# Batch 0's squares first, four norm products, q scales through DRAM, and another order of loads, in a channel-attention and MLP kernel

## The chip, the cores and the metric

The kernel runs on one core of one Trainium2 chip. The metric is the device time of one execution in microseconds (us), as the median of several runs. Differences of about 0.2% (4.3 us) are what a measurement of this kernel can tell from no change.

## The reference

Four batches of `q`, `k`, `v` with 6080 rows and 256 channels go through channel attention, and its result through a two-layer MLP of width 2048 with an activation that is a clipped square:

```python
qn = q / (norm(q, axis=1) + 1e-6);  kn = k / (norm(k, axis=1) + 1e-6)   # (B, N, C)
s = kn.transpose(0, 2, 1) @ qn / tau                                    # (B, C, C)
a = softmax(s, axis=-1)
x = (v @ a).reshape(B * N, C)
h = x @ w_in
g = where(h >= 1, h, where(h <= -1, 0, (h + 1)**2 / 4))
out = g @ w_out
```

All is float32. The norms run over the 6080 rows, so a batch's softmax needs its whole Gram matrix `k^T q` and the sums of the squares of all its `k` and `q`.

## The kernel before

`v @ a @ w_in` is computed as `v @ (a @ w_in)`, so per batch the kernel makes a matrix W for each of 8 parts of the hidden width (`make_W`, `make_W2`), and then runs 48 blocks (6 pairs of row tiles times 8 parts). A block (`h_ops`, `o_ops`) multiplies W by pieces V of `v` with a seven-product scheme for 2x2 blocks, applies the activation on ScalarE and VectorE, and multiplies by `w_out`. Every product of two float32 numbers is made of three fp32r matmuls of a high and a low half (`mm3`, line 452). There are 192 blocks in all.

An `Order` object collects all operations with an engine, an estimated duration and a due time, and then writes out the order of the instructions by a list schedule: at each step the engine that can start first takes, among the operations that are ready by then, the one with the lowest due time. Due times at or below -1000 (`URGENT`) may also hold their engine up to 0.6 us. After that each engine runs its instructions in the order written, and so does SP's queue of DMAs, which issues every load and store. An instruction whose input is late holds up all behind it on its engine.

The start of the program is a stage of its own. Batch 0's Gram matrix is made from 13 chunks of `kq` (lines 807 to 834) with plain fp32 matmuls (line 818): a chunk has 4 row groups (the first and the last one 2), a row group 2 matmuls of 128x256, and each such matmul stands as two rows in the trace. Four buffers of 1 MB hold chunks, and each becomes free when TensorE and ScalarE have read it. ScalarE squares each chunk in pieces of 1024 columns (lines 826 and 832) and VectorE adds the pieces up in `mh_mem` (line 833, 23 additions). `norm_sums` (line 839) then sums over the partitions with 8 matmuls against one column of ones. `softmax` (line 499) follows: a copy, a power on GpSimd, three small VectorE steps, then the scales of `q` as a row on all partitions (lines 524 to 535: multiply the identity by the scales, multiply by a matrix of ones on TensorE, copy back), the scaled matrix, its maximum, the exponential, four transposes, and the halves of `eT`. `make_W` and the first block come next. The softmax of the other three batches runs inside the blocks of the batch before them, 7 blocks from its end.

Beside that chain the start has work with no link to it: 7 chunks of batch 1's Gram matrix, line 818 too, which TensorE takes as filler (`FILL`, `FSTEP` are its due times), and `convert` (lines 394 to 422), which turns 8 blocks of `w_in` and 8 of `w_out` into halves. One conversion is 3 instructions on ScalarE and 6 on VectorE, and needs one of five `raw` buffers until it has read the block. The list `STARTUP` gives for each block, and for the first V, a due time and the chunk after whose load its own load may be issued. In every batch V needs two `raw` buffers.

Of the kernel before, what the change touches and what calls it, by code (L numbers as in the profile page):

```python
# [8 lines left out]
F32 = mybir.dt.float32  # L9
# [3 lines left out]
AF = mybir.ActivationFunctionType  # L13
ALU = mybir.AluOpType
AX = mybir.AxisListType
P = 128
# [33 lines left out]
URGENT = -1000.0  # L50
# [8 lines left out]
class Order:  # L59
# [28 lines left out]
    def op(self, eng, dur, fn, r=(), w=(), due=0.0, gates=(), size=0, other=None, psum=False, plain=False):  # L88

        o = Op()  # L90
        o.eng, o.dur, o.fn, o.due, o.gates, o.size = eng, dur, fn, due, [g for g in gates if g], size
        o.psum, o.plain = psum, plain
        o.alts = {eng: (dur, fn)}
        if other:
            o.alts[other[0]] = other[1:]
        o.start = o.end = None
        deps = []
        for b in r:
            if b.writer is not None:
                deps.append(b.writer)  # L100
        for b in w:
            deps += b.readers
            if b.writer is not None:
                deps.append(b.writer)
        for b in r:
            b.readers.append(o)
        for b in w:
            b.readers, b.writer = [], o
        o.bufs = list({id(b): b for b in (*r, *w)}.values())
        o.bufs += list({id(b.pool.all): b.pool.all for b in o.bufs if b.pool and b.pool.all}.values())  # L110
        for b in o.bufs:
            b.users.append(o)
            b.left += 1
        o.deps = list({id(d): d for d in deps if d is not o}.values())
        o.next, o.n = [], len(self.ops)
        self.ops.append(o)
        return o
# [114 lines left out]
def act_us(n):  # L232
    return 0.095 + 0.00083 * n


def dve_us(n):
    return 0.067 + 0.00104 * n
# [6 lines left out]
def pool_us(n):  # L244
# [10 lines left out]

EARLY = 7
STARTUP = (
    ('v', 0, -478.3, 15),
    ('out', 5, -462.9, 17),
    ('out', 0, -306.5, 11),  # L260
    ('in', 2, -105.4, 16),
    ('in', 0, -82.1, 7),
    ('in', 1, -62.6, 6),
    ('out', 1, -4.4, 16),
    ('out', 6, 123.4, 7),
    ('out', 2, 163.6, 13),
    ('out', 7, 334.1, 17),
    ('out', 3, 371.7, 3),
    ('out', 4, 467.6, 12),
)  # L270
V_SPREAD = 2.5
WARM = 8
STORE = 15
IN3 = False
WIN_DUE = 41.7
W_DUE = -16.6
FILL = 16.7
FSTEP = -0.13
FIRST = 10
V1 = -7.1  # L280
V1S = 23.8
TAU = 0

# [1 line left out]
def channel_attention_moe(ctx: ExitStack, tc: tile.TileContext, kq, kqT, vT, tau, w_in, w_out, outT):  # L287
# [12 lines left out]
    nc = tc.nc  # L300
    B, N, _, C = kq.shape
# [77 lines left out]
    pools["h22"].held = [acc_all]  # L379
    pools["win2"].held = [win_all]  # L380
    win_dram = [dram.tile([P, 2 * WIN], U32, name=f"win_d{i}") for i in range(FP // 2)]
    w_dram = [[dram.tile([P, WSZ], U32, name=f"w_d{b}_{i}") for i in range(FP)] for b in range(B)]

    ctx.enter_context(tc.manual_schedule())

    def buf(pool):
        return Buf(pools[pool])

    def load(b, src, dst, due, size, gates=(), r=()):
        return op("SP", 0.45, lambda: nc.sync.dma_start(out=dst(), in_=src()), r=r, w=[b], due=due, gates=gates,  # L390
                  size=size)
# [96 lines left out]
    def square_piece(b, s, ct, k, due, gates):  # L488
# [7 lines left out]
                                                               accum_out=st.ssq.ap[:, j:j + 1]),  # L496
           w=[rb, st.ssq], due=due)

    def softmax(b, due):

        st = sts[b]
# [15 lines left out]
        op("DVE", 0.1, lambda: V.tensor_scalar(out=nrm()[:, :CT], in0=nrm()[:, :CT], scalar1=tau_sb[:, 1:2], scalar2=None,  # L517
                                              op0=ALU.mult), r=[tau_buf], w=[c], due=due)
        op("DVE", 0.1, lambda: V.reciprocal(rn(), nrm()), w=[c], due=due)
        d, q, s = (buf("y") for _ in range(3))  # L520
        dd = lambda: d.ap[:, :CT * P].rearrange("p (i c) -> p i c", i=CT)
        ss = lambda: s.ap.rearrange("p (i c) -> p i c", i=CT)
        for ct in range(CT):
            op("DVE", 0.25, lambda ct=ct: V.tensor_scalar(out=dd()[:, ct, :], in0=ident,
                                                         scalar1=rn()[:, CT + ct:CT + ct + 1], scalar2=None,
                                                         op0=ALU.mult), r=[c], w=[d], due=due)
        z = buf("Z")

        def scales():
            od.uneven(3)  # L530
            for ct in range(CT):
                nc.tensor.matmul(z.ap[:, ct * P:(ct + 1) * P], lhsT=ones, rhs=dd()[:, ct, :], start=True, stop=True)  # L532

        op("PE", 0.7, scales, r=[d], w=[z], due=due + 3)
        op("DVE", 0.42, lambda: V.tensor_copy(q.ap[:, :C], z.ap[:, :C]), r=[z], w=[q], due=due + 3)
        gm = (lambda: st.g.ap) if b else (lambda: st.g.ap.rearrange("p (i c) -> p i c", i=CT))
        for it in range(CT):
            op("DVE", 0.42, lambda it=it: V.scalar_tensor_tensor(
# [268 lines left out]
    def big_chunk(i, b, r0, p, T):  # L807
        rb, g = Buf(kq_early), (st.g, g1)[b]
        due = at(0.87 * (r0 // P) + 4) if b == 0 else FILL + FSTEP * (i - n0)
        kq_ops.append(load(rb, lambda: kq[b, r0:r0 + p * T].rearrange("(p t) s c -> p (t s c)", t=T),  # L810
                           lambda: rb.ap[:p, :T * 512], due - 25 if b == 0 else at(56), p * T * 2048,
                           [kq_ops[n0 - 1]] if b else ()))
        last = i == (n0 if b == 0 else len(big)) - 1
        for t in range(T):
            def mm(t=t):
                for it in range(CT):
                    k0 = t * 512 + it * P
                    nc.tensor.matmul(g.ap[:, it * C:(it + 1) * C], lhsT=rb.ap[:p, k0:k0 + P],
                                     rhs=rb.ap[:p, t * 512 + C:t * 512 + 2 * C], start=(r0 == 0 and t == 0 and it == 0),
                                     stop=(last and t == T - 1 and it == CT - 1), skip_group_check=True)  # L820

            op("PE", CT * 0.433, mm, r=[rb], w=[g], due=due, plain=True)
        if b:
            return
        if i == 0:
            op("ACT", act_us(1024), lambda: nc.scalar.activation(acc.ap, rb.ap[:, :1024], AF.Square), r=[rb], w=[acc],
               due=due)
            return
        for t in range(0, T, 2):
            src = lambda t=t: rb.ap[:p, t * 512:t * 512 + 1024]  # L830
            sq = Buf(sq_early)
            op("ACT", act_us(1024), lambda sq=sq, src=src: nc.scalar.activation(sq.ap[:p], src(), AF.Square), r=[rb], w=[sq], due=due)  # L832
            op("DVE", dve_us(1024), lambda sq=sq: nc.vector.tensor_tensor(  # L833
                out=acc.ap[:p], in0=acc.ap[:p], in1=sq.ap[:p], op=ALU.add), r=[sq], w=[acc], due=due)

    def norm_sums():
        for j in range(2 * CT):
            for h in range(2):
                nc.tensor.matmul(st.pt.ap[:, j:j + 1], lhsT=acc.ap[:, h * 512 + j * P:h * 512 + (j + 1) * P],
                                 rhs=ones[:, 0:1], start=(h == 0), stop=(h == 1))  # L840

    def mark_b():

# [10 lines left out]
       w=[tau_ps], due=at(TAU), plain=True)  # L854
    op("DVE", 0.1, lambda: nc.vector.tensor_copy(tau_sb[:, 1:2], tau_ps.ap[:, 0:1]), r=[tau_ps], w=[tau_buf], due=at(TAU))
    st.pt = buf("Z")
    op("PE", 1.84, norm_sums, r=[acc], w=[st.pt], due=URGENT - 20, plain=True)
    softmax(0, URGENT - 20)
    sts[1].g = buf("gacc")
    op("DVE", dve_us(512), lambda: nc.vector.tensor_copy(sts[1].g.ap.rearrange("p i c -> p (i c)"), g1.ap), r=[g1],  # L860
# [73 lines left out]
```

## Time and profile before

| | |
|---|---|
| median of 3 runs | 2154.58 us (2154.46 to 2154.76) |
| profiled execution, its own time | 2155.51 us |
| span in the profile, first to last instruction | 2153.7 us |
| TensorE busy | 2148.7 us of the span |
| VectorE busy | 1785.9 us |
| ScalarE busy | 1634.4 us |
| GpSimd busy | 5.1 us |
| mean granted TensorE clock | 0.999 |

A row of the timeline gives the start, the time covered, the engine, line, operation, the tiles written and read, and how many instructions are merged in it. Matmuls are pipelined, so a single one shows a duration longer than the time after which the next may start: a run of rows covers (number - 1) x pace + the duration of the last. What TensorE loses is therefore read from the starts of runs and not from its busy time. In the lists of engines PE is TensorE's matmuls, DVE VectorE, ACT ScalarE, POOL GpSimd, and SPq the DMA queue of SP.

### The profile page before, as it was taken

The page shows a single profiled execution, that of the slowest core. Times are in us where ns is not written, and L with a number is a line of the kernel's source. Part 1 is how long each engine was busy: PE and PEld are TensorE (multiplying, and loading weights), DVE is VectorE, ACT ScalarE, POOL GpSimd, SP SyncE. Part 2 cuts the span into 40 slices and gives each one's busy share as a digit, 9 for nine tenths or more (in the row PEclk, how much of TensorE's full clock was granted, in tenths as well). Part 3 has the DMA queues.
Part 4 walks back from the last instruction along what each step waited for, and adds up shares of the span by engine and source line. Part 5 has one row for each costly group of instructions (what it writes and reads, how often), then busy time and mean ns, then how long its engine had stood idle before and what let it go on. Part 6 is the DMA issues. An engine that isn't in the chain of part 4 may idle for free.

```text
span 2153.7 us, 27733 instructions
## 1 busy us (share of the span) xinstructions
PE 2148.7 (100%) x9949; PEld 1811.1 (84%) x9949; DVE 1785.9 (83%) x3125; ACT 1634.4 (76%) x2926; POOL 5.1 (0%) x12
## 2 busy tenths in 40 slices
PE   9999999999999999999999999999999999999999
PEld 8888888888888888888888888888888888888887
DVE  8897877888888888888888888888888878878776
ACT  7798877776788777777778877777767777766766
POOL 0000000000000000000000000000000000000000
PEclk9999999999999999999999999999999999999999
DMA  9755445454255444444425445454443432332331
GB/s 381 275 189 188 150 157 173 142 174 148 84 210 190 164 166 152 177 161 161 146 102 211 163 159 183 152 194 152 153 144 118 151 125 91 126 125 100 125 118 37
DMA packets 81467, 340.09 MB, mean 158 GB/s; under 512 B 8370, under 2 KB 16690, under 8 KB 77490
## 3 DMA queue, kind: packets, MB, share of 16 engines
q1 hardware_dynamic: 81330, 338.33, 44.3%
q8 instruction: 78, 1.28, 0.2%
q14 instruction: 59, 0.48, 0.1%
HBM read 279.84 MB, written 58.46 MB: 157 GB/s over the span
## 4 chain that ended last, share of the span: by engine, by line
PE 96%; DVE 2%; DMA 2%; ACT 1%; issue 0%; SPq 0%; DVEq 0%; ACTq 0%
PE bank L452 96%; DMA raw<-w_in 1%; DVE mh_mem L833 1%; DMA raw<-w_out 0%; DMA kq<-kq 0%; ACT u L405 0%; DVE u L415 0%; ACT u L408 0%; DVE sf_mem L575 0%; DVE u L710 0%; ACT sf_mem L832 0%; DVE w_mem L581 0%; DVE u L419 0%; DVE u L406 0%; PE bank L532 0%
## 5 line engine op out<-in xcount | busy, mean ns | idle before, releaser
L452 PE MATMUL bank<-x,wout 128*128 128x512 f32 (+1 forms) x3951 | 1012.9, 387 | 0.2 <-DVE x L714 0.2
L452 PEld LDWEIGHTS bank<-x,wout 128*128 128x128 f32 x3951 | 738.2, 188 | 143.6 <-DVE x L714 0.6
L452 PE MATMUL bank<-v,w_mem 128*128 128x512 f32 (+1 forms) x3264 | 846.5, 387 | 0.0
L452 PEld LDWEIGHTS bank<-v,w_mem 128*128 128x128 f32 x3264 | 611.8, 188 | 120.9 <-DVE u L710 0.5
L710 DVE SCALAR_TENSOR_TENSOR u<-bank,u 128x512 f32<-128x512 f32 (+1 forms) x576 | 391.8, 681 | 236.1 <-ACT u L708 235.3
L706 ACT ACTIVATE u<-bank 128x512 f32<-128x512 f32 (+1 forms) x576 | 342.9, 595 | 226.2 <-PE bank L452 214.3
L708 ACT ACTIVATE u<-u 128x512 f32<-128x512 f32 (+1 forms) x768 | 459.7, 624 | 9.4
L714 DVE TENSOR_TENSOR x<-u,x 128x512 fp32r<-128x512 f32 (+1 forms) x658 | 439.6, 681 | 11.0 <-ACT x L712 4.0
L712 ACT CAST x<-u 128x512 fp32r<-128x512 f32 (+1 forms) x363 | 224.1, 619 | 136.4 <-DVE u L710 134.9
L452 PE MATMUL bank<-x,w_mem 128*128 128x512 f32 (+1 forms) x768 | 207.4, 387 | 0.0
L452 PE MATMUL bank<-g,wout 128*128 128x512 f32 (+1 forms) x660 | 183.7, 387 | 0.0
L452 PEld LDWEIGHTS bank<-x,w_mem 128*128 128x128 f32 x768 | 144.0, 188 | 28.3
L737 DVE TENSOR_TENSOR bank<-bank,mh_mem 128x512 f32<-128x512 f32 (+1 forms) x192 | 132.3, 689 | 24.8 <-PE bank L452 23.8
L452 PEld LDWEIGHTS bank<-g,wout 128*128 128x128 f32 x660 | 123.2, 188 | 23.7
L713 DVE CAST x<-u 128x512 fp32r<-128x512 f32 (+1 forms) x295 | 123.4, 422 | 15.1 <-DVE u L710 0.5
L741 DVE TENSOR_TENSOR mh_mem<-bank,mh_mem 128x512 f32<-128x512 f32 (+1 forms) x192 | 130.8, 681 | 5.5 <-PE bank L452 0.3
L710 DVE SCALAR_TENSOR_TENSOR u<-mh_mem,u 128x512 f32<-128x512 f32 (+1 forms) x192 | 129.7, 676 | 0.4 <-ACT u L708 0.4
L706 ACT ACTIVATE u<-mh_mem 128x512 f32<-128x512 f32 (+1 forms) x192 | 118.9, 619 | 0.0
L732 ACT COPY mh_mem<-bank 128x512 f32<-128x512 f32 (+1 forms) x192 | 110.4, 575 | 6.4 <-PE bank L452 2.2
L734 ACT COPY bank<-bank 128x512 f32<-128x512 f32 (+1 forms) x192 | 110.8, 577 | 4.0 <-PE bank L452 0.5
L452 PEld LDWEIGHTS bank<-kqs 128*128 128x128 f32 (+1 forms) x696 | 91.2, 191 | 4.4
L452 PE MATMUL bank<-kqs 128*128 128x256 f32 (+1 forms) x696 | 92.6, 283 | 0.0
(98 smaller groups left out, 1262.1 us busy)
## 6 DMA issues: line engine op xcount, KB each, us to landing
w_mem<-w_d SPq DMA_DIRECT2D x160, 896.0 KB, 4.6
raw<-kqT SPq DMA_DIRECT2D x60, 512.0 KB, 5.6
w_d<-w_mem SPq DMA_DIRECT2D x32, 896.0 KB, 4.5
raw<-kq SPq DMA_DIRECT2D x55, 512.0 KB, 5.4
kq<-kq SPq DMA_DIRECT2D x18, 1024.0 KB, 8.9
raw<-vT SPq DMA_DIRECT2D x32, 512.0 KB, 6.5
win_mem<-win_d SPq DMA_DIRECT2D x12, 1024.0 KB, 4.9
outT<-y_mem SPq DMA_DIRECT2D x32, 256.0 KB, 2.2
```

The source lines that it names most:

```text
L452: nc.tensor.matmul(out, lhsT=lhs(a), rhs=rhs(c), start=start and m == 0, stop=stop and m == 2, skip_group_check=skip)
L706: op("ACT", act_us(n), lambda: nc.scalar.activation(us(), src(), AF.Relu, bias=0.5, scale=0.5), r=[h], w=[u], due=d_sat)
L708: op("ACT", act_us(n), lambda: nc.scalar.activation(us(), us(), AF.Square), w=[u], due=d_sq)
L710: op("DVE", dve_us(n), lambda: nc.vector.scalar_tensor_tensor(out=us(), in0=src(), scalar=1.0, in1=us(), op0=ALU.max, op1=ALU.min), r=[h], ...
L712: op("ACT", act_us(n), lambda: nc.scalar.copy(t.ap[:, 0, :n], us()), r=[u], w=[t], due=d_hi, other=("DVE", dve1_us(n), lambda: nc.vector.t ...
L713: other=("DVE", dve1_us(n), lambda: nc.vector.tensor_copy(t.ap[:, 0, :n], us())) if g >= FIRST else None)
L714: op("DVE", dve_us(n), lambda: nc.vector.tensor_tensor(out=t.ap[:, 1, :n], in0=us(), in1=f32(t.ap[:, 0, :n]), op=ALU.subtract), r=[u], w=[ ...
L732: op("ACT", act_us(n), lambda: nc.scalar.copy(m5.ap[:, :n], a.ap[:, :n]), r=[a], w=[m5], due=d - U)
L734: op("ACT", act_us(n), lambda: nc.scalar.copy(a.ap[:, :n], z.ap[:, :n]), r=[z], w=[a], due=d - U)
L737: op("DVE", dve_us(n), lambda: nc.vector.tensor_tensor(out=bb.ap[:, :n], in0=z.ap[:, :n], in1=m5.ap[:, :n], op=ALU.add), r=[z, m5], w=[bb] ...
L741: op("DVE", dve_us(n), lambda: nc.vector.tensor_tensor(out=h22.ap[:, :n], in0=z.ap[:, :n], in1=m5.ap[:, :n], op=ALU.add), r=[z, m5], w=[h2 ...
L833: op("DVE", dve_us(1024), lambda sq=sq: nc.vector.tensor_tensor(out=acc.ap[:p], in0=acc.ap[:p], in1=sq.ap[:p], op=ALU.add), r=[sq], w=[acc ...
```

## The change

- All squares of batch 0, and their additions, get a due time 174.9 units earlier (`SQ`): from about -83 (first chunk) to -21 (last) to about -258 to -196. They stay behind the `URGENT` operations.
- The two halves of the sum of squares are first added on VectorE (one addition of 512 columns), and `norm_sums` has 4 matmuls in place of 8.
- For batches 1 to 3 the row of q scales is no longer made on VectorE and TensorE: SP stores the two columns of scales to DRAM and loads them back as one row on all partitions. Batch 0 keeps the old way (`scale_row`).
- The list of startup loads has another order, other due times and other gates, V's operations are spread wider (5.6 for 2.5), and the constants beside it differ; the filler's due times are 10.9 + 2.0 per chunk in place of 16.7 - 0.13 per chunk, and conversions may run on ScalarE or VectorE from block 6 on where it was block 10 (`FIRST`, the copies of the activation's high half).

```diff
 STARTUP = (
-    ('v', 0, -478.3, 15),
-    ('out', 5, -462.9, 17),
-    ('out', 0, -306.5, 11),
-    ('in', 2, -105.4, 16),
-    ('in', 0, -82.1, 7),
-    ('in', 1, -62.6, 6),
-    ('out', 1, -4.4, 16),
-    ('out', 6, 123.4, 7),
-    ('out', 2, 163.6, 13),
-    ('out', 7, 334.1, 17),
-    ('out', 3, 371.7, 3),
-    ('out', 4, 467.6, 12),
+    ('out', 5, -594.8, 11),
+    ('v', 0, -339.2, 15),
+    ('out', 0, -291.1, 12),
+    ('in', 2, -267.0, 12),
+    ('in', 1, -214.8, 6),
+    ('out', 6, -4.6, 10),
+    ('in', 0, 33.3, 5),
+    ('out', 1, 64.7, 11),
+    ('out', 2, 349.6, 13),
+    ('out', 7, 452.2, 14),
+    ('out', 4, 528.7, 7),
+    ('out', 3, 665.7, 5),
 )
-V_SPREAD = 2.5
+V_SPREAD = 5.6
 WARM = 8
-STORE = 15
+STORE = 17
 IN3 = False
-WIN_DUE = 41.7
-W_DUE = -16.6
-FILL = 16.7
-FSTEP = -0.13
-FIRST = 10
-V1 = -7.1
-V1S = 23.8
-TAU = 0
+WIN_DUE = 209.6
+W_DUE = -18.0
+FILL = 10.9
+FSTEP = 2.0
+FIRST = 6
+V1 = -8.7
+V1S = 22.7
+TAU = 10
+SQ = -174.9
...
+    row_dram = [dram.tile([CT, P], F32, name=f"row_d{b}") for b in range(B)]
...
+        if b == 0:
+            scale_row(b, c, q, rn, due)
+        else:
+            row = Buf(ap=row_dram[b])
+            op("SP", 0.45, lambda: nc.sync.dma_start(out=row_dram[b].rearrange("i p -> p i"), in_=rn()[:, CT:]), r=[c],
+               w=[row], due=due, size=1024)
+            load(q, lambda: row_dram[b].rearrange("(o i) p -> o (i p)", o=1).broadcast_to([P, C]), lambda: q.ap[:, :C],
+                 due, 128 * 1024, r=[row])
...
     def norm_sums():
         for j in range(2 * CT):
-            for h in range(2):
-                nc.tensor.matmul(st.pt.ap[:, j:j + 1], lhsT=acc.ap[:, h * 512 + j * P:h * 512 + (j + 1) * P],
-                                 rhs=ones[:, 0:1], start=(h == 0), stop=(h == 1))
+            nc.tensor.matmul(st.pt.ap[:, j:j + 1], lhsT=acc.ap[:, j * P:(j + 1) * P], rhs=ones[:, 0:1], start=True,
+                             stop=True)
...
-    op("PE", 1.84, norm_sums, r=[acc], w=[st.pt], due=URGENT - 20, plain=True)
+    op("DVE", dve_us(512), lambda: nc.vector.tensor_tensor(out=acc.ap[:, :512], in0=acc.ap[:, :512],
+                                                           in1=acc.ap[:, 512:], op=ALU.add), w=[acc], due=URGENT - 20)
+    op("PE", 0.92, norm_sums, r=[acc], w=[st.pt], due=URGENT - 20, plain=True)
```

In the chunks of batch 0, `due=due` of the squares and of their additions becomes `due=due + SQ`. `scale_row` holds the lines 523 to 535 of before, unchanged.

## Rows read from the trace of the kernel before

**Rows 1.** The page, its head and part 1: the span, and the busy time of each engine (share of the span, number of instructions).

```profile
span 2153.7 us, 27733 instructions
PE 2148.7 (100%) x9949; PEld 1811.1 (84%) x9949; DVE 1785.9 (83%) x3125; ACT 1634.4 (76%) x2926; POOL 5.1 (0%) x12
```

**Rows 2.** The page, part 4: the chain of work that ended last, shares of the span by engine.

```profile
PE 96%; DVE 2%; DMA 2%; ACT 1%; issue 0%; SPq 0%; DVEq 0%; ACTq 0%
```

**Rows 3.** The timeline of TensorE up to the first softmax (start, time covered, engine, line, operation, tiles, number of rows merged, idle time before). The second row, from a narrower window, is the last part of the first.

```profile
17.92 30.85 PE L818 MATMUL bank<-kq 128*128 128x256 f32 x140
...
39.75 9.02 PE L818 MATMUL bank<-kq 128*128 128x256 f32 x41
49.00 2.08 PE L839 MATMUL bank<-ones,mh_mem 128*128 128x1 f32 x16 [0.24 <-DVE mh_mem L833]
50.94 7.84 PE L818 MATMUL bank<-kq 128*128 128x256 f32 x28
58.62 0.61 PE L532 MATMUL bank<-y,ones 128*128 128x128 f32 x4
```

**Rows 4.** Busy time of each engine by stretch; behind the engines stand the granted TensorE clock (1.00 is 2.4 GHz), the DMA share and GB/s.

```profile
50.00:51.00 1.00, 1.00 (x10) 1.00 (x9) 1.00 (x2) 1.00 (x2) 0.00 (x0) 0.84 0.94 363
51.00:52.00 1.00, 1.00 (x4) 0.82 (x4) 0.97 (x5) 1.00 (x3) 0.57 (x1) 0.50 0.95 293
...
54.00:55.00 1.00, 1.00 (x6) 0.83 (x5) 0.89 (x5) 0.00 (x0) 0.00 (x0) 0.95 1.03 369
```

**Rows 5.** The timeline of TensorE from the making of W to the first blocks.

```profile
65.36 3.22 PE L452 MATMUL bank<-win_mem,eT 128*128 128x256 f32 x24
...
72.55 1.74 PE L452 MATMUL bank<-v,w_mem 128*128 128x512 f32 x6
74.13 1.89 PE L818 MATMUL bank<-kq 128*128 128x256 f32 x8
75.67 1.73 PE L452 MATMUL bank<-v,w_mem 128*128 128x512 f32 x6
...
78.67 1.55 PE L452 MATMUL bank<-v,w_mem 128*128 128x512 f32 x6
80.07 5.34 PE L818 MATMUL bank<-kq 128*128 128x256 f32 x24
85.06 2.40 PE L452 MATMUL bank<-v,w_mem 128*128 128x512 f32 x9
...
87.98 0.39 PE L452 MATMUL bank<-x,wout 128*128 128x512 f32 x1
88.55 0.73 PE L452 MATMUL bank<-x,wout 128*128 128x512 f32 x2 [0.19 <-DVE x L714]
```

**Rows 6.** VectorE's groups of instructions from 0 to 50 us, and below them one of ScalarE's (line, engine, operation, tiles, shapes, number; busy us, mean ns of one; idle before them). Line 833 is the additions of squares, line 415 stands once in each conversion, line 832 is squares.

```profile
L833 DVE TENSOR_TENSOR mh_mem<-mh_mem,sf_mem 128x1024 f32<-128x1024 f32 x11 | 13.4, 1219 | 0.4
L833 DVE TENSOR_TENSOR mh_mem<-mh_mem,y_mem 128x1024 f32<-128x1024 f32 x11 | 13.4, 1219 | 8.2 <-ACT y_mem L832 8.0
L415 DVE SCALAR_TENSOR_TENSOR u<-raw,u 128x512 uint32<-128x512 uint32 x6 | 4.1, 683 | 0.0
...
L832 ACT ACTIVATE y_mem<-kq 128x1024 f32<-128x1024 f32 (+1 forms) x12 | 12.7, 1056 | 4.2 <-DMA kq<-kq 2.9 <-DVE mh_mem L833 1.4
```

**Rows 7.** The timeline of SP's queue: the issue of batch 0's last chunk, and of the first V.

```profile
34.15 0.33 SPq L390 DMA_DIRECT2D kq<-kq  x1
...
46.62 0.94 SPq L390 DMA_DIRECT2D raw<-vT  x2
```

**Rows 8.** The DMA issues from 30 to 50 us: the last chunk of batch 0 is the only one of 384 KB, and the last column is the time from issue to landing in us.

```profile
kq<-kq SPq DMA_DIRECT2D x1, 384.0 KB, 9.0
```

**Rows 9.** The timeline of all engines in batch 0's softmax: the copy of the sums, the power, the first of the three small steps, the identity times the scales, the first step of V, and the first scaled half of the matrix.

```profile
51.12 0.16 DVE L509 COPY cols<-bank 128x4 f32<-128x4 f32 x1
...
51.43 1.22 POOL L514 TENSOR_TENSOR cols<-cols,half 128x4 f32<-128x4 f32 x1 [49.98 <-DVE cols L509]
...
54.24 0.16 DVE L515 TENSOR_SCALAR cols<-cols 128x4 f32<-128x4 f32 x1
...
54.92 0.48 DVE L524 TENSOR_SCALAR y<-ident,cols 128x128 f32<-128x128 f32 x2
...
57.07 0.69 DVE L662 TENSOR_TENSOR t<-raw,raw 128x512 f32<-128x512 f32 x1 [1.67 <-DMA raw<-vT]
...
59.72 0.48 DVE L538 SCALAR_TENSOR_TENSOR y_mem<-bank,cols,y 128x256 f32<-128x256 f32 x1
```

**Rows 10.** The timeline of TensorE around batch 1's scales (line 532), inside the blocks of batch 0.

```profile
516.92 1.48 PE L452 MATMUL bank<-x,wout 128*128 128x496 f32 x6
...
518.24 0.60 PE L532 MATMUL bank<-y_mem,ones 128*128 128x128 f32 x4
...
519.38 0.85 PE L452 MATMUL bank<-v,w_mem 128*128 128x512 f32 x3
...
520.07 1.50 PE L452 MATMUL bank<-x,wout 128*128 128x512 f32 x6
```

**Rows 11.** The tile eT from 500 to 640 us: its first readers and its last writer (number, durations in ns, first and last start). Below it, the row of SP's queue that follows batch 1's scales.

```profile
L452 PE MATMUL bank<-win_mem,eT x48: 389/389/400, 562.2 to 639.6; 128*128 128x512 f32 x48
...
L563 DVE TENSOR_TENSOR eT<-bank,eT x1: 691/691/691, 528.6 to 528.6; 128x512 fp32r<-128x512 f32 x1
...
523.30 0.43 SPq L390 DMA_DIRECT2D win_mem<-win_d  x1
```

More of the change, by code (lines that the diff above doesn't have):

```diff
@@ L497, in square_piece, with scale_row, scales @@
            w=[rb, st.ssq], due=due)
+    def scale_row(b, c, q, rn, due):
+        d, z = buf("y"), buf("Z")
+        dd = lambda: d.ap[:, :CT * P].rearrange("p (i c) -> p i c", i=CT)
+        for ct in range(CT):
+            op("DVE", 0.25, lambda ct=ct: nc.vector.tensor_scalar(
+                out=dd()[:, ct, :], in0=ident, scalar1=rn()[:, CT + ct:CT + ct + 1], scalar2=None, op0=ALU.mult),
+               r=[c], w=[d], due=due)
+        def scales():
+            od.uneven(3)
+            for ct in range(CT):
+                nc.tensor.matmul(z.ap[:, ct * P:(ct + 1) * P], lhsT=ones, rhs=dd()[:, ct, :], start=True, stop=True)
+        op("PE", 0.7, scales, r=[d], w=[z], due=due + 3)
+        op("DVE", 0.42, lambda: nc.vector.tensor_copy(q.ap[:, :C], z.ap[:, :C]), r=[z], w=[q], due=due + 3)
     def softmax(b, due):
@@ L519, in softmax @@
         op("DVE", 0.1, lambda: V.reciprocal(rn(), nrm()), w=[c], due=due)
-        d, q, s = (buf("y") for _ in range(3))
-        dd = lambda: d.ap[:, :CT * P].rearrange("p (i c) -> p i c", i=CT)
+        q, s = buf("y"), buf("y")
         ss = lambda: s.ap.rearrange("p (i c) -> p i c", i=CT)
[L523 to L535, printed above, removed]
+        if b == 0:
[6 more added lines that the diff above has]
+                 due, 128 * 1024, r=[row])
         gm = (lambda: st.g.ap) if b else (lambda: st.g.ap.rearrange("p (i c) -> p i c", i=CT))
@@ L826, in big_chunk @@
             op("ACT", act_us(1024), lambda: nc.scalar.activation(acc.ap, rb.ap[:, :1024], AF.Square), r=[rb], w=[acc],
-               due=due)
+               due=due + SQ)
             return
@@ L831, in big_chunk @@
             sq = Buf(sq_early)
-            op("ACT", act_us(1024), lambda sq=sq, src=src: nc.scalar.activation(sq.ap[:p], src(), AF.Square), r=[rb], w=[sq], due=due)
+            op("ACT", act_us(1024), lambda sq=sq, src=src: nc.scalar.activation(sq.ap[:p], src(), AF.Square), r=[rb], w=[sq],
+               due=due + SQ)
             op("DVE", dve_us(1024), lambda sq=sq: nc.vector.tensor_tensor(
-                out=acc.ap[:p], in0=acc.ap[:p], in1=sq.ap[:p], op=ALU.add), r=[sq], w=[acc], due=due)
+                out=acc.ap[:p], in0=acc.ap[:p], in1=sq.ap[:p], op=ALU.add), r=[sq], w=[acc], due=due + SQ)
     def norm_sums():
         for j in range(2 * CT):
-            for h in range(2):
-                nc.tensor.matmul(st.pt.ap[:, j:j + 1], lhsT=acc.ap[:, h * 512 + j * P:h * 512 + (j + 1) * P],
-                                 rhs=ones[:, 0:1], start=(h == 0), stop=(h == 1))
+            nc.tensor.matmul(st.pt.ap[:, j:j + 1], lhsT=acc.ap[:, j * P:(j + 1) * P], rhs=ones[:, 0:1], start=True,
+                             stop=True)
     def mark_b():
```

## The prediction

> **What bounds the kernel now.** I read the page first, then the chain of waits, then TensorE's timeline run by run. The page has TensorE busy for 2148.7 of 2153.7 us [rows 1], and the chain that ended last lies on it for 96% [rows 2]. Busy time hides small losses, because a pipelined matmul lasts longer than the step to the next one, so I look at paces. In the blocks six fp32r matmuls of 496 columns start 1.32 us before what follows them, 0.22 each, and three of 512 columns take 0.69, 0.23 each [rows 10]: this is columns over 2.4 GHz with next to nothing between. So from about 90 us on TensorE is the bound, and work of the other engines, or its removal there, is worth nothing. Two things can move the end: matmuls taken off TensorE, and the time it loses in the first 90 us.
>
> The second is small, and the rows show all of it. Filler and Gram rows run at 0.216 (41 rows cover 9.02; less the 0.38 of one, 8.64 over 40) [rows 3]. (a) The last Gram row before the norm product starts at 39.75 + 9.02 - 0.38 = 48.39, and the next could start at 48.61; the norm product starts at 49.00, behind VectorE's last addition: 0.4 us lost. (b) The norm product holds TensorE from 49.00 to 50.94, 1.94 us for 8 matmuls of one column [rows 3]. (c) Right behind it the granted clock falls from 1.00 to 0.50 (1.2 GHz) until shortly after 54 [rows 4]; 28 Gram rows take 7.84 us where 27 x 0.216 + 0.38 = 6.2 is their time: 1.65 us lost. (d) Six block matmuls behind filler take 1.74, elsewhere 1.55: 0.19 for each return from plain fp32, and there are four returns (65.36, 72.55, 75.67, 85.06) [rows 5]: 0.76. (e) One block matmul starts at 88.55 where the pace wanted 88.21, waiting for VectorE [rows 5]: 0.34. (f) The 140 rows from 17.92 cover 30.85 where 139 x 0.216 + 0.38 = 30.4 [rows 3]: 0.45, chunks that landed late. Together 3.6 us beside the product itself. The cold start is left alone.
>
> **The change part by part.** *Four norm products.* Half of 1.94 us goes: -0.97. TensorE does not wait out the new addition, 0.67 us if 512 columns take what 128x512 operations take (line 662, 0.69) [rows 9], if it lies under Gram matmuls; at the present place it would be paid in full (bounds of the term: -1.0 to -0.3).
>
> *Squares first.* VectorE makes 23 additions of 1.22 us, 28 us in all [rows 6], between 8 and 49 us; in the rest it got through about six conversions. Their due times go from -83 to -21 to -258 to -196, so only `out` 5, V, `out` 0 and `in` 2 stand ahead of them, whose loads are gated to the chunks 11 to 15; nearly all additions now wait only for their chunk. The last chunk is issued at 34.15 and lands 9.0 later, at 43.2 [rows 7, 8]. One square (1.06) and one addition (1.22) [rows 6] end at 45.5, the fold at 46.2; one conversion taken before them (by the code's durations 2.5 us of VectorE) makes that 48.7. TensorE has Gram rows of batch 0 until 48.6. So the product moves ahead of the end of the Gram matrix, or to it, and loss (a) should go; but the written order counts 1.13 us for an addition that takes 1.22, so the product may stand on TensorE before its input is there. I take -0.2 for the wait (bounds -0.4, and +1.0, ten additions' drift). The conversions displaced are the same instructions later, on engines that are off the path as long as TensorE has filler. This cover I price under the rivals.
>
> From the product's start the softmax needs 51.12 - 49.00 - 0.97 = 1.15 to the copy, 0.31 to the power, 1.22 for it, then 0.68 (54.24 to 54.92) and 0.56 to the scales' matmuls, 1.1 to line 538 (58.62 to 59.72): 5.0 us [rows 3, 9]. From 46.2 that is 51.3, where line 538 stands at 59.72. Some 8 us of chain go, yet not off the end: TensorE did filler in them, and that filler must be done anyway. What is gained is filler left over for 72 to 90 us, where (e) lies. I take -0.2 there (bounds -0.34, and +1.0 where the first blocks meet more unfinished conversions).
>
> *The clock.* The fall came behind a product of 1.94 us with a wait of 0.4 in front, 2.3 us with almost no columns [rows 3, 4]. No shorter break shows one: the scales' 0.6 us at 58.62 [rows 3] and the break at 88 [rows 5] are followed by rows at full pace. With 0.97 us between full Gram matmuls the stretch lies between 0.6, which cost nothing, and 2.3, which cost 1.65. It is nearer to 0.6, so I take the whole -1.65 (bounds -1.65 and 0).
>
> The Trainium skill ("TensorE: Matmul & The Clock Gate", Part 1) says that the gate follows how busy TensorE has been and lets the clock down after idleness, and its section on HAM oscillation puts this down to waits for DMA. Here TensorE had a matmul issued at nearly all times, and the longest wait was 0.4 us; the trace so agrees with the two levels and not with idleness as the only cause. Taken strictly, the rule makes the wait and not the number of products decide: then halving them gives nothing back, and what that would cost is the second rival.
>
> *q scales through DRAM, batches 1 to 3.* On TensorE 518.24 to 519.38 is 1.14 us, of which three matmuls of 512 columns take 0.68: the scales' part costs 0.46. Behind it 12 matmuls run 512 columns wide where 496 are wanted (`od.uneven(3)`), 0.0067 each, 0.08 [rows 10]. That is -0.54 per batch and -1.6 in three (bounds -1.6 and -1.3, as the transposes set the width too). Two multiplications and a copy leave VectorE too, worth nothing there. What is added: a store of 1 KB in pieces of 4 bytes and a load, each issued by SP, the load waiting for the store. No row shows such a pair. Its ends are nothing and two landings of 9.0 as in the crowded start [rows 8], 18 us; I take the high end, since it changes nothing. The cover: eT is written at 528.6 + 0.7 and first read at 562.2 [rows 11], 33 us. So no wait. Behind the load on SP stand the loads of W and of w_in at 523.3 [rows 11]. W loads are gated to four blocks ahead (line 875), a block being 2153.7 / 192 = 11.2 us, so 18 us of hold-up are covered as well. Were the cover gone, each us would be a us of TensorE, three times.
>
> *Order of loads, due times, filler.* DMA is full at 0.90 to 1.03 [rows 4] and moves the same bytes. The early chunks get fewer blocks between them up to chunk 5 and more at 10 to 12. Loss (f) may shrink or grow (bounds -0.45, +1.0; I take 0). Filler spread over later due times may bring more returns, at 0.19 each (bounds -0.4, +0.8; I take 0).
>
> Sum: -0.97 - 0.2 - 0.2 - 1.65 - 1.6 = -4.6 us. The profiled execution has 2153.7 of span and 1.8 around it, so 2155.5 would become 2150.9, span 2149.1. The median lies 0.9 under the profiled run, and 2154.6 - 4.6 = 2150.0.
>
> **The rivals.** *More of the start's losses go.* With (e), (f) and half of (d) gone as well, -0.1 - 0.45 - 0.4 more: 2149.0, and with (a) whole 2148.8. For it: the softmax ends 8 us sooner. Against: DMA stays full.
>
> *The clock still falls, or TensorE waits at the product.* Either gives back 1.0 to 1.65, and both 2.6: 2151.0 to 2152.6. For it: the clock fell without an idle TensorE, and VectorE's additions run 0.09 longer than written. Against: slack of 2.4 us (46.2 to 48.6), where no conversion comes first.
>
> *The round trip is not free.* Where the pair takes so long that a W load on SP comes late by 0.5 us in each batch, the 1.6 are lost: 2151.6. Against: 45 us of lead, and 33 of cover.
>
> *TensorE runs dry between 70 and 95 us: slower.* V needs two of the five `raw` buffers, and conversions now wait behind squares, so the buffers may still be held when V's load is due (46.62 now, V's first step at 57.07 [rows 7, 9]). Group matmuls start at 72.55; the filler left then is 32 rows, 6.9 us [rows 5]. If V comes x later than its 57.07, TensorE loses x - 6.9 at most. Against a gain of 4.6, the kernel is slower at all from x = 11.5 and by over 0.2% from x = 15.8, V at 73 us. At x = 17 it gives 2155.5 and at x = 21 2159.5. For it: five buffers, and about as many conversions ahead. Against: by 49 us VectorE has had the same additions in both kernels, so as many conversions are done by then, and `v` comes second in due time.
>
> **How the numbers follow.** What can be told from no change is 0.2%, 4.3 us: 2150.3 and 2158.9. The forecast, 2149.0 to 2151.2, has 0.50; it straddles 2150.3, and I count 0.35 below it and 0.15 above. More of the losses gone: 0.10, faster. Clock or wait: 0.22, same. Round trip: 0.03, same. TensorE dry: 0.15, of which 0.07 is within and 0.08 slower. Faster 0.45, same 0.47, slower 0.08. The range leaves out the dry case beyond 2153.4 and a little below: 2147.8 to 2153.4. Should the likeliest one hold, it is 2149.0 to 2151.2.
>
> **What would show it.** The norm product: x8 rows, about 1 us, at 45 to 48 us, with Gram rows of batch 0 before and behind it and no idle time named. The clock: no stretch at 0.50 between 45 and 60. Line 532: 4 rows instead of 16. Line 538 near 51 to 53. eT's readers with no wait for it. Filler still there after 85. It is wrong if a stretch at 0.50 stands behind the product, if TensorE's runs between 60 and 100 show gaps with DMA or VectorE named, or if blocks after 500 us wait for `w_mem`.

## The result and the profile after

The changed kernel takes 2175.68 us (2174.47 to 2176.91) where the kernel before took 2154.53 in the same comparison: slower by 1.0%, ratio 1.0098 with a 95% interval of 1.0082 to 1.0114. The forecast was 2150.0, in a range of 2147.8 to 2153.4. The page of the profile after (span, busy time, and the chain that ended last by engine and by line) reads:

```profile
span 2175.1 us, 27700 instructions
PE 2154.7 (99%) x9929; PEld 1813.1 (83%) x9929; DVE 1787.6 (82%) x3125; ACT 1633.1 (75%) x2918; POOL 5.2 (0%) x12
...
PE 94%; DMA 3%; DVE 1%; ACT 0%; issue 0%; POOL 0%; SPq 0%; ACTq 0%; DVEq 0%; POOLq 0%
PE bank L454 92%; PE bank L830 2%; DMA row_d<-cols 1%; DMA kq<-kq 1%; DMA y_mem<-row_d 1%; DMA raw<-kqT 0%; DMA y<-row_d 0%; DVE mh_mem L846 0%; DVE u L722 0%; DVE x L726 0%; PE bank L857 0%; ACT y_mem L844 0%; DVE w_mem L593 0%; DVE mh_mem L753 0%; DVE g L726 0%
```

The span grew by 21.4 us, and TensorE's busy time by 6.0 only [rows 1]. The chain now runs through `row_d`, the trip through DRAM [rows 2 for before]. Who waits for it, from the list of waits (engine and line waiting, for what: us in total, times, longest):

```profile
PEld bank L454 <- DVE bank L749: 15.5, 4, 7.5
PE bank L454 <- DVE bank L749: 14.1, 3, 7.1
...
DVE y_mem L550 <- DMA y_mem<-row_d: 8.1, 1, 8.1
DVE y_mem L550 <- DMA y<-row_d: 7.7, 1, 7.7
...
DVE y L550 <- DMA y_mem<-row_d: 2.1, 1, 2.1
```

So VectorE waits three times for the row of scales, once in each softmax of batches 1 to 3, and TensorE waits for VectorE. Batch 2's trip, on VectorE's timeline:

```profile
1023.10 0.18 DVE L537 RECIPROCAL cols<-cols 128x4 f32<-128x4 f32 x1
...
1028.92 0.67 DVE L683 TENSOR_TENSOR v<-t,v 128x496 fp32r<-128x496 f32 x1
1037.70 0.48 DVE L550 SCALAR_TENSOR_TENSOR y_mem<-gacc,cols,y_mem 128x256 f32<-128x256 f32 x1 [8.12 <-DMA y_mem<-row_d]
1038.10 0.67 DVE L674 TENSOR_TENSOR t<-raw,t 128x496 f32<-128x496 f32 x1
1038.69 0.68 DVE L749 TENSOR_TENSOR bank<-bank,mh_mem 128x496 f32<-128x496 f32 x1
```

The scales are ready at 1023.28. The first scaled half (line 550) stands on VectorE directly behind 1028.92 and waits there 8.12 us, till 1037.70. Line 749, a sum that every block needs, stands two places behind it and needs nothing of the softmax. SP's queue in the same stretch:

```profile
1023.31 0.38 SPq L544 DMA_DIRECT2D row_d<-cols  x1
1031.73 0.32 SPq L392 DMA_DIRECT2D y_mem<-row_d  x1
1032.15 14.09 SPq L392 DMA_DIRECT2D w_mem<-w_d  x2
```

The store of 1 KB holds the load back from 1023.31 to 1031.73, and the load lands at 1037.7: 8.4 and 6.0 us, 14.4 in all. And TensorE:

```profile
1030.83 1.48 PE L454 MATMUL bank<-x,wout 128*128 128x496 f32 x6
1039.42 2.85 PE L454 MATMUL bank<-v,w_mem 128*128 128x496 f32 x6 [7.11 <-DVE bank L749]
1042.06 2.51 PE L454 MATMUL bank<-x,wout 128*128 128x496 f32 x6
1044.41 1.48 PE L454 MATMUL bank<-v,w_mem 128*128 128x496 f32 x6
```

It stops for 7.11 us, and then its first twelve matmuls take 2.85 and 2.51 where six take 1.48. The granted clock (the third column from the end) shows why:

```profile
1034.00:1036.00 2.00, 0.00 (x0) 0.00 (x0) 0.00 (x0) 0.00 (x0) 0.00 (x0) 1.00 0.89 63
1036.00:1038.00 2.00, 0.00 (x0) 0.00 (x0) 0.30 (x1) 0.00 (x0) 0.00 (x0) 0.85 0.90 271
1038.00:1040.00 2.00, 0.58 (x2) 0.51 (x3) 2.00 (x5) 1.11 (x3) 0.00 (x0) 0.50 0.45 190
...
1042.00:1044.00 2.00, 2.00 (x6) 1.60 (x5) 1.97 (x6) 2.00 (x5) 0.00 (x0) 0.50 0.00 0
```

The clock fell to 1.2 GHz in the stop and came back past 1044. From 1030.83, 18 matmuls at 0.22 would end their issue at 1034.79 and the next run begins at 1044.41: 9.6 us lost in batch 2's softmax. Batch 3's shows the same picture, 9.9 us read in the same way (24 matmuls from 1572.55, the next run at 1587.72), and batch 1's a smaller one without a fall of the clock, 1.7 us behind a wait of 2.1 on VectorE (24 matmuls from 503.06, the next run at 510.09). Together that is 21.2 us, as much as the kernel lost.

The start did not go as forecast either. TensorE, then ScalarE's last square and VectorE's last two additions, answering to [rows 3]:

```profile
17.20 30.65 PE L830 MATMUL bank<-kq 128*128 128x256 f32 x140
48.82 1.05 PE L851 MATMUL bank<-ones,mh_mem 128*128 128x1 f32 x8 [0.97 <-DVE mh_mem L869]
49.73 13.16 PE L830 MATMUL bank<-kq 128*128 128x256 f32 x52
...
45.72 1.06 ACT L844 ACTIVATE y_mem<-kq 96x1024 f32<-96x1024 f32 x1 [2.38 <-DMA kq<-kq]
...
46.81 1.22 DVE L846 TENSOR_TENSOR mh_mem<-mh_mem,y_mem 96x1024 f32<-96x1024 f32 x1 [1.02 <-ACT y_mem L844]
48.07 0.69 DVE L869 TENSOR_TENSOR mh_mem<-mh_mem 128x512 f32<-128x512 f32 x1
```

The last chunk's square waits for its landing until 45.72, where the forecast had 43.2; addition and fold end at 48.76. TensorE waits 0.97 us with its Gram rows done, and the product takes 0.91 (49.73 - 48.82) in place of 1.94. The clock falls all the same, as in [rows 4]:

```profile
51.00:52.00 1.00, 1.00 (x4) 0.83 (x3) 1.00 (x4) 1.00 (x2) 0.55 (x1) 0.50 1.00 414
```

### The profile page after: what moved, and what is told of

It reads as the page before. It is cut to its first block, busy times and chain, and to the rows that moved or that the text cites. A ratio compares the mean times of both kernels' runs of the same rounds, so it can differ in the third digit from the quotient of the medians.

```text
span 2175.1 us, 27700 instructions
## 1 busy us (share of the span) xinstructions
PE 2154.7 (99%) x9929; PEld 1813.1 (83%) x9929; DVE 1787.6 (82%) x3125; ACT 1633.1 (75%) x2918; POOL 5.2 (0%) x12
## 3 DMA queue, kind: packets, MB, share of 16 engines
q1 hardware_dynamic: 82578, 338.73, 43.5%
## 4 chain that ended last, share of the span: by engine, by line
PE 94%; DMA 3%; DVE 1%; ACT 0%; issue 0%; POOL 0%; SPq 0%; ACTq 0%; DVEq 0%; POOLq 0%
PE bank L454 92%; PE bank L830 2%; DMA row_d<-cols 1%; DMA kq<-kq 1%; DMA y_mem<-row_d 1%; DMA raw<-kqT 0%; DMA y<-row_d 0%; DVE mh_mem L846 0%; DVE u L722 0%; DVE x L726 0%; PE bank L857 0%; ACT y_mem L844 0%; DVE w_mem L593 0%; DVE mh_mem L753 0%; DVE g L726 0%
## 5 line engine op out<-in xcount | busy, mean ns | idle before, releaser
L724 ACT CAST x<-u 128x512 fp32r<-128x512 f32 (+1 forms) x352 | 217.2, 618 | 141.7 <-DVE u L722 140.4
L725 DVE CAST x<-u 128x512 fp32r<-128x512 f32 (+1 forms) x306 | 128.3, 423 | 15.1
```

Source lines behind the costliest of these rows:

```text
L724: op("ACT", act_us(n), lambda: nc.scalar.copy(t.ap[:, 0, :n], us()), r=[u], w=[t], due=d_hi, other=("DVE", dve1_us(n), lambda: nc.vector.t ...
L725: other=("DVE", dve1_us(n), lambda: nc.vector.tensor_copy(t.ap[:, 0, :n], us())) if g >= FIRST else None)
```

## The experiments

The theory to begin with: the trip through DRAM costs the time, because its first reader stands on VectorE, which runs its instructions in the order written, some 9 us before its input lands. Rivals: the new order of loads and squares costs it; or the trip costs by itself, through SP's queue or its traffic. The kernel before was timed beside each set of runs, 69 times in all: 2155.12 us beside the first four, 2155.02 and 2155.06 beside the others. Ratios are to these.

**Trip taken out of the changed kernel** (`a_no_trip`).

```diff
-        if b == 0:
+        if True:
             scale_row(b, c, q, rn, due)
```

> The changed kernel, with the q scales of batches 1 to 3 made on VectorE and TensorE as before. Theory: the three trips through DRAM cost the time. TensorE's starts after the three trips show 7.3 + 2.6, 6.9 + 3.7 and some 2.2 us lost, 22 in all, less the 1.6 us of matmuls saved, so this run takes 2175.7 - 21 = 2153 to 2155 us, and waits of VectorE for row_d are gone. Rival: the other order of loads and squares spreads through the whole written order and costs the time; then this run stays above 2165.

Measured: 2154.59 us (2153.13 to 2155.91), ratio to before 0.9996 (0.9987 to 1.0006). The trip is the whole loss. What is left of the change, with its new order, is no different from the kernel before.

**Trip put into the kernel before** (`b_trip`): `row_dram`, `scale_row` and the two branches of the change, and nothing else.

> The kernel before, with the trip through DRAM in batches 1 to 3 and nothing else. Theory (trips): slower by 10 to 21 us, 2165 to 2176, according to what VectorE has queued behind each wait, and the clock drops to 0.50 after long ones. Rival (order of loads and squares): 2153, the 1.6 us of matmuls saved.

Measured: 2179.51 us (2178.41 to 2181.90), ratio 1.0115 (1.0100 to 1.0130): 24 us slower, above the 10 to 21 that was expected. From both sides the trip makes the loss, and the rival of the order falls.

**Same trip, true durations in the schedule** (`a_trip_timed`). The list schedule counted 2.4 us for the store and 2.7 for the load. Here it adds 5.9 and 3.5 to the ends of these two operations.

```diff
-                o.end = dma + self.DMA_END
+                o.end = dma + self.DMA_END + o.late
...
-               w=[row], due=due, size=1024)
+               w=[row], due=due, size=1024, late=5.9)
...
-                 due, 128 * 1024, r=[row])
+                 due, 128 * 1024, r=[row], late=3.5)
```

> The changed kernel, with the two transfers of the trip entered into the list schedule with the durations that the trace shows: 8.3 us for the store and 6.2 for the load where it counted 2.4 and 2.7. Nothing that runs is taken away, only its place in the order moves. Theory A: the cost is the place of the first scaled half on VectorE, written some 9 us before its input; then the waits on row_d fall under 1 us each and the time is 2151 to 2153. Theory B: the trip costs by itself, by SP's queue held up or by its traffic; then 2160 or more stays.

Measured: 2155.94 us (2154.13 to 2157.11), ratio 1.0002 (0.9992 to 1.0011). The same work is still done, and TensorE's order is the same row for row; only VectorE, ScalarE and SP have some rows in other places (and one copy has gone from VectorE to ScalarE). Batch 2's trip now, SP's queue first, then VectorE's first scaled half, then TensorE:

```profile
1022.46 0.38 SPq L544 DMA_DIRECT2D row_d<-cols  x1
1025.55 0.32 SPq L392 DMA_DIRECT2D w_mem<-w_d  x1
1032.35 0.32 SPq L392 DMA_DIRECT2D y_mem<-row_d  x1
...
1038.49 0.48 DVE L550 SCALAR_TENSOR_TENSOR y_mem<-gacc,cols,y_mem 128x256 f32<-128x256 f32 x1 [0.23 <-DMA y_mem<-row_d]
...
1031.30 1.48 PE L454 MATMUL bank<-v,w_mem 128*128 128x496 f32 x6
1032.62 1.48 PE L454 MATMUL bank<-x,wout 128*128 128x496 f32 x6
```

The trip takes as long as before (16.0 us from store to reader), a load of W slips in between store and load, VectorE waits 0.23 us, and TensorE runs on at its pace. Theory A holds: the place in the order cost 19.7 us, not the trip. (The place of W's load has moved too; but in the changed kernel no wait of TensorE names `w_mem`.) The time stays above the 2151 to 2153 expected, so the saved matmuls do not show.

**Pieces of 8 bytes** (`a_trip_8b`), order as in the changed kernel.

```diff
-    row_dram = [dram.tile([CT, P], F32, name=f"row_d{b}") for b in range(B)]
+    row_dram = [dram.tile([P, CT], F32, name=f"row_d{b}") for b in range(B)]
...
-            op("SP", 0.45, lambda: nc.sync.dma_start(out=row_dram[b].rearrange("i p -> p i"), in_=rn()[:, CT:]), r=[c],
+            op("SP", 0.45, lambda: nc.sync.dma_start(out=row_dram[b], in_=rn()[:, CT:]), r=[c],
...
+                in1=q.ap[:, :C].rearrange("x (p i) -> x i p" if b else "x (i p) -> x i p", i=CT), op0=ALU.mult,
```

> The changed kernel, with the scales stored as 128 pieces of 8 bytes in place of 256 of 4, and read in that order; order written as in the changed kernel. If the store's 8.2 us go by the number of pieces, it lands after 4.5 to 5 us, each of VectorE's waits is 3.5 shorter, and the time is 2164 to 2168. If they go by the bytes or are a fixed latency, the store keeps 8 us and the time stays at 2174 to 2177.

Measured: 2157.50 us (2155.57 to 2158.59), ratio 1.0010 (1.0000 to 1.0019). All engines and SP's queue run their rows in the order of the changed kernel, the load of W behind the trip too. The store lands after 3.2 us, less than half of 8.2, and two waits of 1.7 and 2.0 on `row_d` are left. The time fell further than expected: when VectorE's wait is short, TensorE still has rows in front of those that need line 749, and stops for 0.8 and 1.1 us (read from the starts of its runs), and no fall of the clock comes with it.

**Pieces of 16 bytes** (`a_trip_16b`), run once: all four columns stored, and read by `q.ap.rearrange("x (p i) -> x i p", i=2 * CT)[:, CT:, :]`.

> The changed kernel with all four columns stored, 128 pieces of 16 bytes, and a load of twice the size. If the store goes by the number of pieces (256: 8.2 us, 128: 3.2), it lands after 3.2 us as with 8 bytes. If it goes by how many pieces share a short stretch of memory, it lands sooner, at 2 to 2.7 us.

**Pieces of 4 bytes, 64 bytes apart** (`a_trip_4b_apart`), run once.

```diff
-    row_dram = [dram.tile([CT, P], F32, name=f"row_d{b}") for b in range(B)]
+    row_dram = [dram.tile([CT * P, 16], F32, name=f"row_d{b}") for b in range(B)]
...
-            op("SP", 0.45, lambda: nc.sync.dma_start(out=row_dram[b].rearrange("i p -> p i"), in_=rn()[:, CT:]), r=[c],
+            op("SP", 0.45, lambda: nc.sync.dma_start(out=row_dram[b].rearrange("(i p) x -> p i x", i=CT)[:, :, 0], in_=rn()[:, CT:]), r=[c],
```

> One look, for the landing of the store alone: 256 pieces of 4 bytes again, each 64 bytes from the next instead of side by side. If pieces that lie side by side hold each other up, the store lands after 1.4 to 3 us. If a piece of 4 bytes is slow by itself, or if the number of pieces counts, it keeps 7 to 9 us. The load now gathers single numbers and will be much slower, so the time of the run, above 2190, says nothing.

Measured for these: the store's line in the changed kernel, with 8 bytes, with 16 bytes, and with 4 bytes apart (issues on SP, and time from issue to landing as min/median/max).

```profile
L544 SPq DMA_DIRECT2D row_d<-cols x3: 377/377/378, 487.7 to 1565.0; - x3
...
DMA to landing us min/median/max: 7.8/8.2/8.4
```

```profile
L544 SPq DMA_DIRECT2D row_d<-cols x3: 327/327/327, 486.4 to 1552.6; - x3
...
DMA to landing us min/median/max: 2.9/3.2/3.3
```

```profile
L544 SPq DMA_DIRECT2D row_d<-cols x3: 326/327/327, 486.7 to 1553.4; - x3
...
DMA to landing us min/median/max: 1.4/1.4/1.4
```

```profile
L544 SPq DMA_DIRECT2D row_d<-cols x3: 377/378/378, 487.9 to 1583.3; - x3
...
DMA to landing us min/median/max: 1.6/1.6/1.6
```

256 pieces of 4 bytes land after 8.2 us side by side and after 1.6 us apart: neither their number nor their size is slow, their lying side by side is (three stores each, in one execution). The run with 16 bytes took 2154.93 us; the one with pieces apart 2201.92, since its load gathers single numbers and takes 21 us.

**Eight-byte trip with its durations in the schedule** (`a_8b_timed`): `a_trip_8b` with `late=1.0` and `late=2.5`.

> The changed kernel with the trip in pieces of 8 bytes, and with both transfers entered into the schedule with the durations that were measured for it (3.4 and 5.2 us). If only the place in the order costs, VectorE's waits on row_d fall from 3.7 us to under 0.5, TensorE's two stops of 0.8 and 1.1 us go, and the time falls from 2157.5 to 2154 to 2156, beside the kernel without the trip (2154.6). A gain of the full 1.1 to 1.6 us of matmuls would give 2153.

Measured: 2153.35 us (2152.78 to 2157.07), ratio 0.9995 (0.9986 to 1.0004). No wait on `row_d` is named any more, as expected. The median lies under the 2154 to 2156 of the expectation, near the 2153 that it gave for the full gain; but the executions spread over 4 us, and the difference from before can't be told from none.

**Norm products against 128 columns** (`a_no_trip_wide`): `a_no_trip` with the sum in 128 columns, of which one is read.

```diff
-            nc.tensor.matmul(st.pt.ap[:, j:j + 1], lhsT=acc.ap[:, j * P:(j + 1) * P], rhs=ones[:, 0:1], start=True,
-                             stop=True)
+            nc.tensor.matmul(st.pt.ap[:, j * P:(j + 1) * P], lhsT=acc.ap[:, j * P:(j + 1) * P], rhs=ones, start=True,
+                             stop=True)
```

> The changed kernel without the trip, with the four norm products against 128 columns of ones in place of one (the same sum in 128 columns; a row takes 0.11 us either way). If the fall of the clock behind the norm product comes from its single columns, no stretch at 0.50 is left near 50 us in any profile, and the time is 1.0 to 1.7 under the kernel without the trip: some 2153. If it comes from the wait in front of it (1.1 us for VectorE) or from neither, the stretch and the 2154.6 stay.

Measured: 2154.01 us (2153.44 to 2154.98), ratio 0.9994 (0.9985 to 1.0003). The product on TensorE's timeline, and the clock behind it:

```profile
49.87 1.16 PE L851 MATMUL bank<-ones,mh_mem 128*128 128x128 f32 x8 [1.14 <-DVE mh_mem L869]
...
51.00:52.00 1.00, 1.00 (x7) 0.87 (x6) 0.94 (x3) 0.54 (x2) 0.62 (x1) 1.00 1.06 442
```

The wait in front of it is as long (1.14, where `a_no_trip` has 1.06), and the clock stays at 1.00. The mean granted clock was 1.000 in all 11 executions. With single columns (`a_no_trip`) it was 0.999 in 5 of 10, and these took 2155.0 to 2155.9 against 2153.1 to 2154.2 for the other five. So in this start a fall goes with some 1.6 us, and it comes in some executions of the same program and not in others; behind 128 columns it came in none. The median gained 0.6 only, less than the 1.0 to 1.7 expected, as half of the executions of `a_no_trip` had no fall to lose.

**The two halves of the start, in the kernel before**: the fold and four products alone (`b_norm4`), squares first alone (`b_sq`), and both (`b_sq_norm4`), each with the lines of the change and the old order of loads.

> The kernel before with the fold and the four norm products alone. Forecast's term: TensorE holds 0.97 us less for the product, and waits 0.4 to 1.1 us for VectorE in front of it, since the fold's 0.7 us is then in the open. So 2154 to 2155 beside 2155.1, no difference that can be told; a full gain of 1 us would need the wait to stay at 0.4.

> The kernel before with batch 0's squares first, nothing else. The forecast had VectorE's last addition at 45.5 us and the product ahead of the end of the Gram matrix; in the changed kernel it stood at 48.0, held by the last chunk's landing at 45.7. So the norm product should start between 46.5 and 48.6, and the time stays within 1 us of 2155.1. If the conversions that are pushed back starve TensorE at 85 to 95 us, it is 2157 to 2162.

> The kernel before with squares first, the fold and four products: the changed kernel but for the trip and for the order of loads and its constants. Together with the kernel without the trip (2154.6) it gives what the order of loads is worth. The four products alone made 2161, with TensorE waiting 2.8 us for a chunk at 62 and for VectorE at 86 to 94. If squares first cures that, 2154 to 2155; if only the order of loads does, 2158 to 2162.

Measured: 2161.18 (2160.65 to 2162.76; ratio 1.0028, 1.0017 to 1.0040), 2160.17 (2158.81 to 2161.88; 1.0024, 1.0015 to 1.0033) and 2161.71 us (2161.39 to 2164.20; 1.0033, 1.0021 to 1.0045). Each is slower by 5 to 7 us. For the first no difference was expected, and for the second none or 2157 to 2162. TensorE in `b_norm4`, then in `b_sq`:

```profile
50.71 8.88 PE L818 MATMUL bank<-kq 128*128 128x256 f32 x40
62.37 5.41 PE L818 MATMUL bank<-kq 128*128 128x256 f32 x16 [2.77 <-DMA kq<-kq]
```

```profile
50.26 10.61 PE L819 MATMUL bank<-kq 128*128 128x256 f32 x48
63.06 4.54 PE L819 MATMUL bank<-kq 128*128 128x256 f32 x12 [2.20 <-DMA kq<-kq]
...
94.64 1.67 PE L453 MATMUL bank<-v,w_mem 128*128 128x512 f32 x6 [0.68 <-DVE bank L738]
```

The filler itself runs dry: TensorE is through the rows in front of a chunk of batch 1 at 59.6 and 60.9 us, and the chunk lands at 62.3 and 63.0. It is not much later than in the kernel before (62.1), where no matmul waits for it; TensorE comes to it sooner. Behind the waits of 2.8 and 2.2 us the matmuls run slowly (16 rows in 5.41 us, where 15 x 0.216 + 0.38 is 3.6; the granted clock is 0.50 from 64 to 66), and waits for VectorE follow up to 97 us. The new order of loads, with its due times and constants, takes these 7 us back (2161.7 to 2154.6, beside 2155.1 for the kernel before both times), and no more. In it four chunks of batch 1 have landed by 56.7 us, in the old order three.

**All three corrections** (`a_16b_timed_wide`): 16-byte trip, durations in the schedule (`late=-0.9` and `2.7`), 128 columns.

> The changed kernel with three corrections: the trip in pieces of 16 bytes (store 1.4 us), both transfers entered into the schedule with their measured durations (1.5 and 5.4 us), and the norm products against 128 columns. Theory: waits on row_d near zero, the mean clock 1.000 in every run, and the 1.1 to 1.6 us of matmuls saved: 2152 to 2153.5, some 2 us or 0.1% under the kernel before. If what the trip saves is used up elsewhere, it ends beside the kernel without the trip and with 128 columns, 2154.0.

Measured: 2153.59 us (2153.26 to 2154.36), ratio 0.9993 (0.9984 to 1.0002), mean clock 1.000 in all 11 executions, no wait on `row_d`: just above the 2152 to 2153.5 expected. All 11 lie under the lowest of 22 of the kernel before (2154.45). The interval still holds 1, so a gain of 0.07% is likely and not shown.

## Why the prediction was wrong, point by point

**q scales through DRAM: the step that failed.** It said "The cover: eT is written at 528.6 + 0.7 and first read at 562.2 [rows 11], 33 us. So no wait." It priced the trip against the last reader of the softmax, and not against what stands behind its first reader on VectorE. The trip took 14 us, inside the 18 that the step allowed. But the schedule counted 5, so line 550 was written where its input was 9 us away, and each block's line 749 behind it held up TensorE. The bounds of the term were -1.6 to -1.3; it measured +21.1 (2175.7 - 2154.6), from stops of up to 7.1 us and the slow clock after two of them. The step named what queued behind the load on SP, and left out the queue of the engine that reads the row. `a_trip_timed` shows that this was 19.7 us of the price; the 1.3 that are left can't be told from none.

**The rival of the round trip** had chance 0.03 and the price of the lost saving only: it looked at W loads on SP. Those were indeed held back (batch 2's to 1032.15, where `a_trip_timed` issues it at 1025.55), and no wait of TensorE for `w_mem` is named; the delay came to it through VectorE's line 749 (and 0.9 us in batch 1 through ScalarE's line 746).

**Squares first.** The step had the product at 46.2, or 48.7 with a conversion first. It started at 48.82, through the last chunk's late landing (45.7 for 43.2). The new order issues two loads of `w_out` just before that chunk and the old one; that they delay it is likely and not shown. Nor would a landing in time have been enough: in `b_sq` the chunk lands at 43.5, and the product starts at 48.45, because VectorE takes its last additions in turn with conversions and starts the last one at 47.19. Counted as loss (a) was, TensorE could go on at 47.69 (17.20 + 30.65 - 0.38 + 0.22), so the wait is 1.13 where it was 0.40: +0.7, near the bound of +1.0, for -0.2.

The softmax behind the product was to reach line 538 in 5.0 us, and took 15.0. GpSimd's power ends at about 51.5. VectorE takes the result up at 58.66, behind other rows written ahead of it, and TensorE makes the scales at 62.72, behind 52 filler rows. The first scaled half starts later than in [rows 9] (59.72):

```profile
58.66 0.16 DVE L533 TENSOR_SCALAR cols<-cols 128x4 f32<-128x4 f32 x1
...
63.83 0.48 DVE L550 SCALAR_TENSOR_TENSOR y_mem<-bank,cols,y 128x256 f32<-128x256 f32 x1
```

This is the omission of the failed step once more: the sum followed the chain and left out the queues of the engines that it runs on. Here TensorE lost nothing by it, since it had filler: no wait of it is named between 60 and 100 us.

**Four norm products.** -0.97 was forecast for the time that the product holds TensorE, and 1.94 became 0.91, -1.03. Together with the longer wait, which is counted above, the product's stretch is 0.3 us shorter.

**The clock.** -1.65 was forecast for a stretch of 0.97 us without full matmuls. The stretch became 1.13 of wait and 0.91 of product, 2.0 us, and the clock fell in the profile of the changed kernel and in half of the executions of `a_no_trip`. So the rival of the clock and the wait came true, both halves of it. In the new start the size was right, some 1.6 us. In the old start, from which the gain was to come, the fall costs nothing that shows: of the 69 executions of the kernel before, 37 had a mean clock below 1.000 and took 2155.3 us on average, and the 32 at 1.000 took 2155.1. The profile of `b_trip` shows what takes the gain back. Its start is the old one, row for row, and the clock did not fall in it. Its TensorE, and below it the transposes in the profile of the kernel before, where the clock fell:

```profile
50.97 6.29 PE L829 MATMUL bank<-kq 128*128 128x256 f32 x28
...
62.49 1.13 PE L829 MATMUL bank<-kq 128*128 128x256 f32 x4 [1.32 <-DMA kq<-kq]
63.46 0.60 PE L567 MATMUL bank<-ident,y_mem 128*128 128x128 f32 x4
```

```profile
63.38 0.60 PE L556 MATMUL bank<-ident,y_mem 128*128 128x128 f32 x4
```

The 28 rows take 6.29 us in place of 7.84 [rows 3], as the step had it. Then TensorE waits 1.32 us for a chunk that lands at 62.45, and the transposes start no sooner than with the fall. The step counted a loss of TensorE without asking whether the next chunk would be there.

**Order of loads.** Taken as 0. On top of the fold and the squares it was worth 7 us, all of them used up by what these two broke; it was not run without them. The whole start came to -0.5 us (2154.59 beside 2155.12, no difference that can be told) for a forecast of -3.0.

**TensorE dry between 70 and 95 us**, the rival on the slow side, did not happen in the changed kernel. Something like it is what `b_norm4` and `b_sq` show, from 60 us on, through a chunk of filler and not through V. Its sums for x = 17 and x = 21 take the gain off twice: 2150.0 + x - 6.9 is 2160.1 and 2164.1, not 2155.5 and 2159.5. The forecast does not rest on them.

Left open: the saved scales' matmuls, some 1.6 us, are not seen. With the waits gone, `a_trip_timed` is 1.3 us above `a_no_trip`, `a_8b_timed` 1.2 below it, and `a_16b_timed_wide` 0.4 below `a_no_trip_wide`; intervals of about 0.1% hold all three. `b_trip` lost 3 us more than the trip costs in the changed kernel: VectorE's three waits for `row_d` add up to 19.9 us there and to 17.9 here, and the rest stays open.

## What to carry to other kernels

When a transfer takes the place of work on an engine, look at the first instruction that reads it, and at what stands behind that on the same engine, before looking at how late the result is needed. In an order written ahead of time a wrong duration costs more than a slow step: the same 14 us trip cost 21 us at the wrong place and nothing that could be told at the right one. And a start that is balanced on loads, filler and conversions is not the sum of its parts: the fold with four products and the earlier squares lost 5 to 6 us each until the loads were put in another order. Time given back to the busiest engine is a gain only if its next input has landed by then.

## What the hardware showed that was not expected

Small pieces that lie side by side in DRAM hold each other up. A store of 256 pieces of 4 bytes landed after 8.2 us side by side and 1.6 us when 64 bytes apart; 128 pieces of 8 bytes took 3.2, of 16 bytes 1.4. The packets of all four are through 1.0 to 1.1 us after the issue; what differs is the time from there to the landing. The Trainium skill ("DMA: Bandwidth & Descriptors", Specifications) says that transfers under 512 bytes are made by reading, changing and writing back. All four are under that, so the rule alone does not tell 8.2 from 1.4; what the trace adds is that neighbours matter.

Whether the clock falls after a thin stretch of work differs between executions of one program. With the new start and products of one column (`a_no_trip`, `a_trip_timed`, `a_trip_8b`, `a_8b_timed`) the mean clock was below 1.000 in 20 of 41 executions, and these took 1.7 to 2.4 us longer than the others of their kernel; with products of 128 columns it was 1.000 in 22 of 22. The Trainium skill ("TensorE: Matmul & The Clock Gate", Part 1) speaks of how busy TensorE is and names idleness. The falls in the stops of 7 us agree; idleness alone does not tell the waits of 1.1 us that a fall followed from the same waits that none followed.
